# Delta-rule attention: the triangular inverse by 16-token substitution with a join on TensorE, both batches in step

## The chip, the cores and the metric

The program runs on one core of a Trainium2 chip. The metric is the device time of one execution in microseconds, measured over several runs; one further execution was profiled. A core has TensorE (PE in the rows, its weight loads PEld), VectorE (DVE), ScalarE (ACT), GpSimd (POOL) and SyncE (SP, which here only issues DMAs). Each engine executes its own instructions in program order and waits on semaphores for the others.

## The reference

Three stages follow each other. The change is in the first. For 2 batches, 8 heads, 768 tokens and 48 channels a state of 48x48 is updated token by token:

```
k_n = k / (norm(k) + 1e-06)
for t in range(768):
    y[t] = q[t] @ state
    state = state + beta[t] * outer(k_n[t], v[t] - k_n[t] @ state)
```

The second stage sends each token to one of 8 experts (the expert of the token before it is kept where a local gate says so) and applies a two-layer feed-forward network; the third is a gated feed-forward network with a convolution over 3 tokens.

## The kernel before, in words

**Blocks.** The 768 tokens are cut into 6 blocks of 128 (tb). Within a block the recurrence is solved at once: with the Gram matrix G of the keys, U = T (V - K S), where T is the inverse of a unit lower triangular matrix made of G and beta. Then the outputs are q S plus a masked Gram product M with U, and the state S gets K^T U. The 16 pairs of batch and head lie on the free axis; where a matrix product works on pairs, a batch b, a head pair i and a half e name one (hh = 8b + 4e + i).

**The inverse.** `solve` inverts the diagonal pieces of 32 tokens by substitution: the pieces are transposed so that 4 x 32 lanes each hold half of one head's row (lines 408 to 429), then 31 steps follow, each a multiply (line 435) and an add (line 437) on at most 136 elements a lane. Blocks 0, 2 and 4 run these steps on VectorE, blocks 1, 3 and 5 on GpSimd. The result is transposed back into Tn and Tt (lines 442 and 445). `merge1` and `merge2` (lines 462 and 475) join pairs of 32 into 64 on TensorE, 32 matmuls of 32x32 each; ScalarE takes the products out (lines 465 and 478).

**The recurrence in a block.** For each batch b: `s_ks` multiplies keys by the state (line 485), `s_r` forms V - K S for 64 tokens (line 504), `s_t` applies the 64x64 inverse (line 513, 8 matmuls on one quadrant of the array, ScalarE copies the result to U at line 515), `s_g` carries the first 64 tokens' U to the second half (line 521), and `s_r` and `s_t` follow for the second half. `s_qs` (line 492) and `s_m` (line 547) give the outputs, `s_s` (line 532) the new state, copied by ScalarE and VectorE (lines 537 and 539). `rows` (line 138) makes the gate's products of the finished block, `route1` to `route4` pick the expert, and an indirect DMA scatters the rows. Every fp32 matmul shows in the trace as two weight loads and two matmul records.

**Order.** The order of all pieces on all engines is written out by hand in the string ORDER: a letter is a piece, the digits its block, batch and half (J a Gram product, n a compaction of the diagonal pieces, A, B, C the start of a substitution, d one step, f its end, u and v the merges, K r t g q s the recurrence, m and x the output, a b e c the routing, w a warming matmul of 512 columns that keeps TensorE busy and gives no result). PSUM tiles of Gram products, merges, gate products and warming matmuls share a ring of 3 banks (tag gps). Loads of keys, queries and values are issued by SyncE ahead of the stage and once per block.

**After the stage** the second and third stages run as before; their first weights are loaded into buffers that the first stage leaves.

Of the kernel before, what the change touches and what calls it, by code (L numbers as in the profile page):

```python
# [9 lines left out]
I32 = mybir.dt.int32  # L10
# [22 lines left out]
THR = -1.5 * 2.0 ** -23  # L33

# [13 lines left out]
def hh_of(b, i, e):  # L48
    return 8 * b + 4 * e + i


class Router:
# [26 lines left out]
    def consts(self, ctx):  # L79
# [39 lines left out]
        self.xT, self.x = {}, {}  # L119
# [13 lines left out]
    def rows(self, tb, b, pg):  # L133

        nc = self.nc
        pt = pg.tile([128, 4, 2 * D + 9], F32, name="ptx", tag="gps")
        for i in range(4):
            nc.tensor.matmul(out=pt[:, i], lhsT=self.xT[b][:, i], rhs=self.wg[:, i], start=True, stop=True)
        if b == 0:
            self.lp = self.sb.tile([128, 2, 9], F32, name="lp", tag="lp", k=tb)  # L140
        nc.vector.tensor_reduce(out=self.lp[:, b], in_=pt[:, :, 2 * D:].rearrange("p i n -> p n i"), axis=AX.X, op=ALU.add)
        if b == 0:
            self.x[tb] = self.sb.tile([128, 2, XW], F32, name="x", tag="x", k=tb)
        x = self.x[tb][:, b, 0:DM]
        nc.scalar.copy(out=x.rearrange("p (i n) -> p i n", i=4), in_=pt[:, :, 0:2 * D])
        t0 = b * SEQ + tb * 128
        nc.sync.dma_start(out=self.xall[t0:t0 + 128, :], in_=x)

    def route1(self, tb, pg):
        nc, sb = self.nc, self.sb  # L150
        lp = self.lp
# [91 lines left out]
class Pieces:  # L243


    def __init__(self, gen):
        self.gen, self.left = gen, 31

    def setup(self):
        next(self.gen)  # L250

    def step(self):
        if self.left:
            next(self.gen)
            self.left -= 1

    def finish(self):
        while self.left:
            self.step()
        for _ in self.gen:  # L260
            pass


class Attention:
# [6 lines left out]
    def __init__(self, ctx, tc, kq, kn, vn, beta, wm):  # L271
# [16 lines left out]
        self.bt = con.tile([128, NTB, 32], F32, name="bt")  # L288
        self.mn = con.tile([128, NTB, 32], F32, name="mn")
        self.warm1 = con.tile([1, 1], F32, name="warm1")  # L290
        nc.vector.memset(self.warm1, 0.0)  # L291
        self.half = con.tile([128, 2], F32, name="half")
        self.ut = con.tile([128, 128], F32, name="ut")
        self.S = con.tile([128, 2, 4, 2, 64], F32, name="S")
        self.U2 = [[con.tile([128, 4, 2, 64], F32, name=f"U{b}{p}") for p in range(2)] for b in range(2)]
        self.sps = self.ps.tile([128, 2, 4, D], F32, name="sps")
        self.KQ, self.KN, self.VN, self.G, self.M, self.As, self.Tt, self.Tn = ({} for _ in range(8))
        self.W, self.Y, self.R, self.P = {}, {}, {}, {}

    def consts(self):  # L300
        nc = self.nc
        nc.scalar.activation(out=self.warm1, in_=self.warm1, func=AF.Sqrt)
        nc.gpsimd.memset(self.ut, 1.0)
        nc.gpsimd.affine_select(out=self.ut, in_=self.ut, compare_op=ALU.is_gt, fill=0.0, base=0,
                                pattern=[[1, 128]], channel_multiplier=-1)
        pi = self.con.tile([128, 1], I32, name="pi")
        nc.gpsimd.iota(pi, pattern=[[0, 1]], base=0, channel_multiplier=1)
        nc.vector.tensor_scalar(out=pi, in0=pi, scalar1=16, scalar2=None, op0=ALU.bitwise_and)
        nc.vector.tensor_scalar(out=self.half[:, 1:2], in0=pi, scalar1=-1.0 / 16, scalar2=None, op0=ALU.mult)
        nc.vector.tensor_scalar(out=self.half[:, 0:1], in0=self.half[:, 1:2], scalar1=-1.0, scalar2=-1.0, op0=ALU.mult, op1=ALU.add)  # L310
# [19 lines left out]
    def vhat(self, tb):  # L330
        m = self.mn[:, tb, 0:16].unsqueeze(2).to_broadcast([128, 16, D])
        self.nc.gpsimd.tensor_tensor(out=self.VN[tb], in0=self.VN[tb], in1=m, op=ALU.mult)

    def gram0(self, which, part):

        nc = self.nc
        dst = self.G if which == 0 else self.M
        if part == 0:
            p = self.gp if which == 0 else self.mp
            dst[0] = p.tile([128, 16, 128], F32, name="GM", tag="GM", k=0)  # L340
        if part % 2:
            return
        b = part // 2
# [17 lines left out]
    def gram(self, tb, part):

        nc = self.nc
        if part % 2:
            return
        if tb not in self.G:
            self.G[tb] = self.gp.tile([128, 16, 128], F32, name="GM", tag="GM", k=tb)
            self.M[tb] = self.mp.tile([128, 16, 128], F32, name="GM", tag="GM", k=tb)
        t = [self.pg.tile([128, 2, 2, 128], F32, name="gps", tag="gps") for _ in range(2)]
        b, i0 = part // 4, part % 4  # L370
# [4 lines left out]
        for e in range(2):  # L375
            h = slice(hh_of(b, i0, e), hh_of(b, i0, e) + 2)
# [10 lines left out]
    def compact(self, tb, q, eng):  # L387

        nc = self.nc
# [3 lines left out]
        o, i = self.As[tb][r], self.G[tb][r, :, 32 * q:32 * q + 32]  # L393
        if eng == "s":
            nc.scalar.copy(out=o, in_=i)
        else:
            {"v": nc.vector, "g": nc.gpsimd}[eng].tensor_copy(out=o, in_=i)

    def solve(self, tb):

        nc = self.nc
        up = self.up
        dve = tb % 2 == 0
        eng = nc.vector if dve else nc.gpsimd
        X = up.tile([128, 32, 16], F32, name="X", tag="X", k=tb)
        (nc.gpsimd if tb == 0 else eng).memset(X, 0.0)
        N = up.tile([128, 32, 32], F32, name="N", tag="N", k=tb)
        nc.vector.transpose(out=N.rearrange("p j (h u) -> p j h u", h=2),
                            in_=self.As.pop(tb).rearrange("p u j -> p j u").unsqueeze(2).to_broadcast([128, 32, 2, 16]))
        yield  # L410
        mu = up.tile([128, 32], F32, name="mu", tag="mu", k=tb)
        cu = up.tile([128, 32], F32, name="cu", tag="cu", k=tb)
        nu = up.tile([128, 32], F32, name="nu", tag="nu", k=tb)

        nc.scalar.activation(out=mu, in_=N.rearrange("p j i -> p (j i)")[:, ::33], func=AF.Sqrt)
        yield
        nc.vector.tensor_scalar(out=mu, in0=mu, scalar1=1e-6, scalar2=None, op0=ALU.add)
        nc.vector.reciprocal(out=nu, in_=mu)
        nc.vector.tensor_tensor(out=cu, in0=self.bt[:, tb], in1=nu, op=ALU.mult)
        nc.vector.scalar_tensor_tensor(out=cu, in0=cu, scalar=-1.0, in1=nu, op0=ALU.mult, op1=ALU.mult)  # L420
        for h in range(2):
            o = X.rearrange("p i l -> p (i l)")[:, 16 * h::33]
            if dve and tb > 0:
                nc.scalar.activation(out=o, in_=cu[:, h::2], func=AF.Copy, scale=self.half[:, h:h + 1])
            else:
                nc.gpsimd.tensor_scalar(out=o, in0=cu[:, h::2], scalar1=self.half[:, h:h + 1], scalar2=None, op0=ALU.mult)

        eng.tensor_tensor(out=N, in0=N, in1=cu.unsqueeze(2).to_broadcast([128, 32, 32]), op=ALU.mult)
        nc.vector.transpose(out=self.mn[:, tb], in_=mu)
        yield  # L430
        tm = up.tile([128, 136], F32, name="tm", tag="tm", k=tb)
        for j in range(31):
            n, m = 31 - j, j // 2 + 1
            t = tm[:, :n * m].rearrange("p (a b) -> p a b", b=m)
            eng.tensor_tensor(out=t, in0=N[:, j + 1:, j:j + 1].to_broadcast([128, n, m]),  # L435
                              in1=X[:, j:j + 1, :m].to_broadcast([128, n, m]), op=ALU.mult)
            eng.tensor_tensor(out=X[:, j + 1:, :m], in0=X[:, j + 1:, :m], in1=t, op=ALU.add)  # L437
            yield
# [702 lines left out]
```

## Time and profile before

| what | us |
|---|---|
| median of 3 runs | 504.63 (502.23 to 511.55) |
| the profiled execution's own time | 503.22 |
| its span, first to last instruction | 501.5 |
| PE busy | 455.2 (91%) |
| DVE busy | 362.8 (72%) |
| ACT busy | 240.4 (48%) |
| POOL busy | 175.4 (35%) |

Busy time is summed over the whole span, so it mixes stages; overlapping matmuls count once. PEclk is the clock that was granted to TensorE as a share of its full speed (1.00 is 2.4 GHz, 0.50 is 1.2 GHz).

### The profile page before, as it was taken

The numbers are of one execution on the slowest core, as the hardware profiler recorded it, in microseconds if no ns is written. First come the engines' busy times: TensorE is split into PE (matmuls) and PEld (weight loads), VectorE is DVE, ScalarE is ACT, GpSimd is POOL, SyncE is SP. The second block draws the span as 40 slices with busy tenths as digits, with TensorE's granted clock in tenths as the row PEclk, the third lists the DMA queues.
The fourth block names the chain that finished last, engine by engine and source line by source line (L and its number), as shares of the span: only waits on it lengthen the run. The fifth ranks groups of instructions, "written<-read, shape, count | busy, mean of one in ns | idle before, by whom it ended". The sixth has DMA issues, their size and how long they took to land. (4 is left out here: it accounts for less than half of the span.)

```text
span 501.5 us, 10035 instructions
## 1 busy us (share of the span) xinstructions
PE 455.2 (91%) x3980; PEld 403.4 (80%) x3982; DVE 362.8 (72%) x711; ACT 240.4 (48%) x435; POOL 175.4 (35%) x319
## 2 busy tenths in 40 slices
PE   7891998998997899988999999999999987999994
PEld 3551686976887698937999999999977987899993
DVE  3879669879669646464886799999812699965491
ACT  3772526347242314335656447546323764456541
POOL 5468828465548543230112202201210022222230
PEclk8787659679689958988999999999999999999998
DMA  9992020020220020169996788674008010002002
GB/s 278 367 371 84 3 61 5 18 80 2 64 67 33 35 95 33 66 225 347 293 316 228 258 314 290 223 256 158 33 31 283 2 33 31 1 0 95 1 1 101
DMA packets 44327, 64.97 MB, mean 130 GB/s; under 512 B 2480, under 2 KB 33456, under 8 KB 44272
## 3 DMA queue, kind: packets, MB, share of 16 engines
q1 hardware_dynamic: 42192, 58.38, 34.8%
q0 software_dynamic: 1792, 5.56, 2.9%
q8 instruction: 33, 0.54, 0.5%
q10 hardware_dynamic: 288, 0.31, 0.2%
q14 instruction: 22, 0.18, 0.1%
HBM read 48.38 MB, written 15.86 MB: 128 GB/s over the span
## 5 line engine op out<-in xcount | busy, mean ns | idle before, releaser
L750 POOL DMA_INDIRECT ys<-y,oi x16 | 25.8, 1615 | 126.5 <-ACT y L747 124.1
L666 DVE TENSOR_TENSOR wl<-raw,wh 128x1536 fp32r<-128x1536 f32 x32 | 56.1, 1754 | 5.2 <-ACT wh L665 5.1
L719 PE MATMUL ph<-xh,wh 128*128 128x256 f32 x192 | 55.1, 287 | 1.6 <-DVE hl L724 0.9
L719 PE MATMUL ph<-xl,wh 128*128 128x256 f32 x192 | 54.6, 285 | 0.3 <-DVE xl L689 0.3
L719 PE MATMUL ph<-xh,wl 128*128 128x256 f32 x192 | 54.6, 284 | 0.0
L928 POOL TENSOR_TENSOR ngl<-nc,ngh 128x768 fp32r<-128x768 f32 x13 | 25.6, 1968 | 82.5 <-ACT ngh L927 79.4
L940 PE MATMUL no<-wout,ngh 128*128 128x384 f32 x192 | 52.0, 343 | 0.0
L665 ACT CAST wh<-raw 128x1536 fp32r<-128x1536 f32 x32 | 47.2, 1475 | 4.9 <-DMA raw<-in_w_dram 4.9
L906 PE MATMUL npt<-nx,win 128*128 128x384 f32 (+1 forms) x243 | 44.2, 333 | 3.5 <-DVE nx L892 2.3
L906 PEld LDWEIGHTS npt<-nx,win 128*128 128x128 f32 x243 | 40.9, 188 | 4.5 <-DVE nx L892 2.7
L738 PE MATMUL py<-wh,hh 128*128 128x384 f32 x128 | 43.6, 341 | 0.0
L855 PE MATMUL warm<-wm 128*128 128x512 bf16 x121 | 40.4, 447 | 2.9 <-DVE warm L291 1.3
L738 PE MATMUL py<-wl,hh 128*128 128x384 f32 x128 | 43.0, 336 | 0.0
L738 PE MATMUL py<-wh,hl 128*128 128x384 f32 x128 | 43.0, 336 | 0.0
L437 POOL TENSOR_TENSOR X<-X,tm 128x126 f32<-128x126 f32 (+22 forms) x93 | 40.2, 432 | 7.3
L719 PEld LDWEIGHTS ph<-xh,wh 128*128 128x128 f32 x192 | 36.9, 192 | 2.4 <-DVE hl L724 1.3
L437 DVE TENSOR_TENSOR X<-X,tm 128x126 f32<-128x126 f32 (+22 forms) x93 | 36.1, 389 | 3.4
L435 POOL TENSOR_TENSOR tm<-N,X 128x126 f32<-128x126 f32 (+22 forms) x93 | 35.8, 385 | 6.2
L719 PEld LDWEIGHTS ph<-xh,wl 128*128 128x128 f32 x192 | 37.4, 195 | 0.0
L719 PEld LDWEIGHTS ph<-xl,wh 128*128 128x128 f32 x192 | 36.9, 192 | 0.5 <-DVE xl L689 0.5
L374 PE MATMUL gps<-kq 64*128 64x256 f32 x160 | 32.4, 471 | 4.7 <-ACT GM L359 3.2
L940 PEld LDWEIGHTS no<-wout,ngh 128*128 128x128 f32 x192 | 35.8, 193 | 0.1
(187 smaller groups left out, 1026.1 us busy)
## 6 DMA issues: line engine op xcount, KB each, us to landing
raw<-in_w_dram SPq DMA_DIRECT2D x32, 768.0 KB, 5.6
kq<-in_kq_dram SPq DMA_DIRECT2D x12, 512.0 KB, 6.5
xs<-S SPq DMA_DIRECT2D x1, 3144.0 KB, 14.6
xe<-xs SPq DMA_DIRECT2D x8, 393.0 KB, 6.9
raw<-in_win_dram SPq DMA_DIRECT2D x6, 512.0 KB, 7.4
raw<-in_wout_dram SPq DMA_DIRECT2D x8, 384.0 KB, 4.9
vn<-in_vn_dram SPq DMA_DIRECT2D x6, 384.0 KB, 3.3
kn<-in_kn_dram SPq DMA_DIRECT2D x6, 384.0 KB
```

The source lines that it names most:

```text
L374: nc.tensor.matmul(out=t[e][:, j], lhsT=kq[:, 0], rhs=kq, start=True, stop=True)
L435: eng.tensor_tensor(out=t, in0=N[:, j + 1:, j:j + 1].to_broadcast([128, n, m]), in1=X[:, j:j + 1, :m].to_broadcast([128, n, m]), op=ALU.mult)
L437: eng.tensor_tensor(out=X[:, j + 1:, :m], in0=X[:, j + 1:, :m], in1=t, op=ALU.add)
L665: nc.scalar.copy(out=h, in_=r)
L666: nc.vector.tensor_tensor(out=l, in0=r, in1=h.bitcast(F32), op=ALU.subtract)
L719: nc.tensor.matmul(out=p[:, j], lhsT=a[:, k, fs], rhs=c[:, k].rearrange("p c t -> p (c t)"), start=(n == 0), stop=(n == 8))
L738: nc.tensor.matmul(out=self.Y[c], lhsT=a[:, j, ts], rhs=w[:, f], start=(f2 == 0 and j == 0 and n == 0), stop=(f2 == 3 and j == 1 and n == 2))
L750: nc.gpsimd.indirect_dma_start(out=self.views[2 * e + c], out_offset=bass.IndirectOffsetOnAxis(ap=I[:, c:c + 1].bitcast(U32), axis=0), in_ ...
L855: nc.tensor.matmul(out=w, lhsT=wm[:, 0:128], rhs=wm, start=True, stop=True)
L906: nc.tensor.matmul(out=p, lhsT=a[:, k, fs], rhs=x[:, k, cs], start=(j == 0), stop=(j == 8))
L928: (nc.vector if (b, f) >= (1, 6) or (b, f) == (0, 0) else nc.gpsimd).tensor_tensor(out=gl, in0=c, in1=gh.bitcast(F32), op=ALU.subtract)
L940: nc.tensor.matmul(out=O[b, t], lhsT=a[:, ts], rhs=w[:, f], start=(f == 0 and j == 0), stop=(f == 7 and j == 2))
```

## The change

- Substitution runs on diagonal pieces of 16 tokens: 15 steps in place of 31, all on VectorE, at most 64 elements a lane for one block. Blocks are grouped as (0), (1, 2), (3, 4), (5); the two blocks of a group share their instructions. GpSimd runs no step.
- Two 16-token inverses are joined to 32 on TensorE: `join1` and `join2` are 64 matmuls each of one block, on the four diagonal 32x32 tiles of the array in turn, with one VectorE instruction between them. `merge1` and `merge2` follow as before.
- In keys, k and v of the second batch the two 64-token halves are swapped on the partitions. The first half of batch 0 lies on partitions 0 to 63, that of batch 1 on 64 to 127. `s_t` and `s_g` issue the matmuls of both batches alternately, `s_r` handles both batches in one instruction of 128 partitions, `s_ks` issues 8 matmuls with 64 weight columns in place of 4 with 128. ScalarE copies U of batch 0, VectorE of batch 1.
- G and M become one tile GM, taken out of PSUM by one copy in place of two; the ring holds 4 blocks in place of 5 and 4.
- ORDER is written anew: 60 warming pieces become 55, 15 of which stand at the end in both.

```diff
+GROUPS = [(0,), (1, 2), (3, 4), (5,)]
...
+def rows_of(g, b):
+    return slice(64, 128) if g ^ b else slice(0, 64)
...
-            nc.scalar.copy(out=self.G[tb][:, h], in_=t[e][:, :, 0])
-            nc.scalar.copy(out=self.M[tb][:, h], in_=t[e][:, :, 1])
+            nc.scalar.copy(out=self.GM[tb][:, h:h + 2], in_=t[e])
...
-        eng = nc.vector if dve else nc.gpsimd
...
-        for j in range(31):
-            n, m = 31 - j, j // 2 + 1
...
+    def step(self, gr, j):
+        nc = self.nc
+        g = len(GROUPS[gr])
+        N, X = self.N[gr], self.X[gr]
+        n, m = 15 - j, j + 1
...
+        nc.vector.tensor_tensor(out=t, in0=N[:, :, j + 1:, j:j + 1].to_broadcast([128, g, n, m]),
+                                in1=X[:, :, j:j + 1, :m].to_broadcast([128, g, n, m]), op=ALU.mult)
+        nc.vector.tensor_tensor(out=X[:, :, j + 1:, :m], in0=X[:, :, j + 1:, :m], in1=t, op=ALU.add)
+
+    def turn(self, tb):
...
+        nc.scalar.activation(out=F[:, 0], in_=X, func=AF.Copy, scale=self.h[:, 0:1])
+        nc.vector.tensor_scalar(out=F[:, 1], in0=X, scalar1=self.h[:, 1:2], scalar2=None, op0=ALU.mult)
...
+        nc.vector.transpose(out=Dn.rearrange("p s u l -> p l s u"), in_=F.rearrange("p s i l -> p l s i"))
+        nc.vector.transpose(out=Dt.rearrange("p u s i -> p i s u"), in_=F.rearrange("p s i l -> p i s l"))
...
+    def join1(self, tb):
...
+        for u in range(16):
+            for q in range(4):
+                r = slice(32 * q, 32 * q + 32)
+                nc.tensor.matmul(out=pp[r, u], lhsT=self.GM[tb][r, hh_u(q // 2, u), 0, r], rhs=Dn[r, 0, u], start=True, stop=True)
+        nc.vector.scalar_tensor_tensor(out=self.PI[:, :, 0:16], in0=pp, scalar=self.h[:, 2:3],
+                                       in1=self.eye[:, 0:16].unsqueeze(1).to_broadcast([128, 16, 16]), op0=ALU.mult, op1=ALU.add)
+
+    def join2(self, tb):
...
+                nc.tensor.matmul(out=po[r, u], lhsT=self.PI[r, u], rhs=Dt[r, u], start=True, stop=True)
+
...
+        nc.scalar.copy(out=Tt[:, :, 32:64], in_=po)
+        nc.scalar.activation(out=Tt[:, :, 0:32], in_=po, func=AF.Copy, scale=self.h[:, 3:4])
...
+        nc.vector.transpose(out=Tn, in_=Tt[:, :, 32:64])
...
+    def s_t(self, tb, g):
...
         for i in range(4):
             for e in range(2):
-                nc.tensor.matmul(out=self.W[b][r, i, e], lhsT=self.Tt[tb][r, hh_of(b, i, e)], rhs=self.R[b][r, i, e],
-                                 start=True, stop=True, skip_group_check=True)
-        nc.scalar.copy(out=self.U2[b][tb % 2][r, :, :, 0:D], in_=self.W[b][r])
...
+                for b in range(2):
+                    r = rows_of(g, b)
+                    nc.tensor.matmul(out=w[r, i, e], lhsT=self.Tt[tb][r, 8 * g + 4 * e + i], rhs=self.R[g][r, i, e],
+                                     start=True, stop=True, skip_group_check=True)
+        for b, copy in ((0, nc.scalar.copy), (1, nc.vector.tensor_copy)):
+            r = rows_of(g, b)
+            copy(out=self.U2[b][tb % 2][r, :, :, 0:D], in_=w[r])
```

VectorE, the end of block 0's substitution, before (tm and X the steps' tiles, Tn and Tt the inverse):

```order
L435 TENSOR_TENSOR tm<-N,X 128x30
L437 TENSOR_TENSOR X<-X,tm 128x2x15
L435 TENSOR_TENSOR tm<-N,X 128x16
L437 TENSOR_TENSOR X<-X,tm 128x16
L442 STREAM_TRANSPOSE Tn<-X 128x32x16
L445 STREAM_TRANSPOSE Tt<-Tn 128x16x32 x2
```

The same place now (F, Dn, Dt the turned 16-token inverses, pq the product of `join1`, PI the weights of `join2`, B and N_562 the start of the group of blocks 1 and 2):

```order
L452 TENSOR_TENSOR tm<-N_301,X_302 128x15
L454 TENSOR_TENSOR X_302<-X_302,tm 128x15
L463 TENSOR_SCALAR F<-X_302,halves 128x256
L466 STREAM_TRANSPOSE Dn<-F 128x16x32
L467 STREAM_TRANSPOSE Dt<-F 128x16x2x16
L479 SCALAR_TENSOR_TENSOR PI<-pq,halves,eye 128x16x16
L409 STREAM_TRANSPOSE B<-As 128x512
L413 SCALAR_TENSOR_TENSOR N_562<-B,halves,Bh 128x256
L495 STREAM_TRANSPOSE Tn<-Tt 128x512
```

The 31st step ended the substitution before and the 15th does now; behind it stand one scaling, two transposes, the product's scaling and, behind part of the next group's start, the transpose that `merge1` needs.

TensorE, from the first use of the state by block 1 to its first `s_t`, before (gps a Gram product, pps and pos the merges):

```order
L492 MATMUL y<-kq,S 128x128 x4
L485 MATMUL w<-S,kq 128x96 x4
L855 LDWEIGHTS wm
L855 MATMUL warm<-wm 128x512
L485 MATMUL w<-S,kq 128x96 x4
L462 MATMUL pps<-Tn,GM 32x32 x32
L374 MATMUL gps<-kq 128x256 x4
L475 MATMUL pos<-Tt,Pm 32x32 x32
L374 MATMUL gps<-kq 128x256 x4
L513 MATMUL w<-R_1036,Tt 64x48 x8
L513 MATMUL w<-R_1061,Tt 64x48 x8
```

The same place now (pq and poq the joins, of blocks 1 and 2 in turn):

```order
L529 MATMUL w<-S,kq 64x96 x8
L377 MATMUL gps<-kq 128x256 x4
L478 MATMUL pq<-Dn,GM 32x16 x64
L377 MATMUL gps<-kq 128x256 x4
L489 MATMUL poq<-Dt,PI 32x32 x64
L478 MATMUL pq<-Dn,GM 32x16 x64
L529 MATMUL w<-S,kq 64x96 x8
L505 MATMUL pps<-Tn,GM 32x32 x32
L489 MATMUL poq<-Dt,PI 32x32 x64
L152 MATMUL ptx<-wg,xT 128x105 x4
L516 MATMUL pos<-Tt,Pm 32x32 x32
L505 MATMUL pps<-Tn,GM 32x32 x32
```

The joins and first merges of two blocks stand together, and block 2's `merge1` too stands ahead of block 1's `s_t`.

TensorE, `s_g` of block 1, before:

```order
L521 MATMUL w<-U_127,GM 64x48 x8
L492 MATMUL y<-kq,S 128x128 x4
L521 MATMUL w<-U_125,GM 64x48 x8
L138 MATMUL ptx<-wg,xT 128x105 x8
L513 MATMUL w<-R_1036,Tt 64x48 x8
```

and now (the four rows of line 571 go on to 16, the two batches' tiles U in turn):

```order
L558 MATMUL w<-R_1071,Tt 64x48 x16
L537 MATMUL y<-kq,S 128x128 x4
L571 MATMUL w<-U_124,GM 64x48
L571 MATMUL w<-U_126,GM 64x48
L571 MATMUL w<-U_124,GM 64x48
L571 MATMUL w<-U_126,GM 64x48
```

Two runs of 8 matmuls, each on one quadrant of the array, have become one run of 16 that changes its quadrant with each matmul.

## Rows read from the trace of the kernel before

**Rows 1.** Busy time by stage: length, then PE, PEld, DVE, ACT, POOL; PEclk, DMA share, GB/s.
```profile
0.00:57.48 57.48, 40.42 (x313) 23.59 (x313) 44.20 (x105) 30.93 (x83) 37.66 (x95) 0.76 0.73 240
57.48:212.77 155.29, 144.15 (x1939) 125.11 (x1939) 110.29 (x285) 63.38 (x137) 81.80 (x177) 0.80 0.14 45
212.77:501.50 288.73, 270.63 (x1731) 254.68 (x1731) 208.28 (x321) 146.06 (x217) 55.97 (x48) 0.97 0.45 153
```

**Rows 2.** Timeline, PE and ACT, 39 to 58 us: start, length, instructions, wait before.
```profile
39.16 1.13 PE L374 MATMUL gps<-kq 64*128 64x256 f32 x6 [0.91 <-ACT GM L359]
49.70 1.91 PE L462 MATMUL pps<-Tn,GM 32*32 32x32 f32 x64 [9.42 <-DVE Tn L442]
...
51.65 1.19 ACT L465 ACTIVATE Pm<-pps 32x512 f32<-32x512 f32 x2 [10.55 <-PE pps L462]
...
55.11 1.70 PE L475 MATMUL pos<-Tt,Pm 32*32 32x32 f32 x64
```

**Rows 3.** Timeline of DVE, the substitution of block 0.
```profile
12.18 1.92 DVE L408 STREAM_TRANSPOSE N<-As 128x1024 f32<-128x1024 f32 x1
...
17.15 0.25 DVE L435 TENSOR_TENSOR tm<-N,X 128x31 f32<-128x31 f32 x1
...
22.75 0.26 DVE L435 TENSOR_TENSOR tm<-N,X 128x96 f32<-128x96 f32 x1
...
41.15 0.46 DVE L435 TENSOR_TENSOR tm<-N,X 128x96 f32<-128x96 f32 x1
...
48.47 1.09 DVE L442 STREAM_TRANSPOSE Tn<-X 128x512 f32<-128x512 f32 x1
```

**Rows 4.** Timeline of POOL, the first step of block 1's substitution.
```profile
32.04 0.25 POOL L435 TENSOR_TENSOR tm<-N,X 128x31 f32<-128x31 f32 x1
```

**Rows 5.** Groups of PE, 57.48 to 212.77 us: count, busy us, mean ns, idle before.
```profile
L513 PE MATMUL w<-R,Tt 64*64 64x48 f32 x384 | 32.4, 248 | 2.5 <-DVE R L504 1.3 <-ACT Tt L478 1.0
L521 PE MATMUL w<-U,GM 64*64 64x48 f32 x192 | 18.3, 263 | 1.5 <-ACT U L515 1.5
...
L374 PE MATMUL gps<-kq 64*128 64x256 f32 x64 | 10.5, 404 | 0.9 <-ACT GM L378 0.9
L855 PE MATMUL warm<-wm 128*128 128x512 bf16 x23 | 10.5, 475 | 0.0
L485 PE MATMUL w<-S,kq 128*128 128x96 f32 x80 | 10.3, 278 | 2.1 <-DVE S L539 2.1
L462 PE MATMUL pps<-Tn,GM 32*32 32x32 f32 x320 | 6.9, 201 | 2.2 <-DVE Tn L442 1.2 <-ACT GM L378 0.8
```

**Rows 6.** Timeline of PE, single pieces while the granted clock is 1.00.
```profile
147.16 2.05 PE L513 MATMUL w<-R,Tt 64*64 64x48 f32 x32 [0.31 <-DVE R L504]
...
159.23 0.92 PE L532 MATMUL sps<-U,kn 128*48 128x48 f32 x32
159.98 1.06 PE L547 MATMUL y<-GM,U 128*64 128x128 f32 x16
...
166.07 1.20 PE L462 MATMUL pps<-Tn,GM 32*32 32x32 f32 x64 [0.96 <-DVE Tn L442]
```

**Rows 7.** Timeline of PE where `s_g` meets `s_t` on another tile, clock 0.50.
```profile
180.72 1.62 PE L521 MATMUL w<-U,GM 64*64 64x48 f32 x13
182.05 0.34 PE L513 MATMUL w<-R,Tt 64*64 64x48 f32 x1
182.15 0.30 PE L521 MATMUL w<-U,GM 64*64 64x48 f32 x1
```

**Rows 8.** Busy time by stretch of half clock, columns as in rows 1.
```profile
59.80:73.40 13.60, 13.60 (x123) 10.96 (x123) 7.37 (x21) 3.85 (x8) 5.27 (x14) 0.50 0.10 30
...
90.50:107.60 17.10, 17.10 (x131) 15.48 (x131) 13.38 (x32) 5.13 (x12) 7.42 (x13) 0.50 0.15 47
...
128.00:141.70 13.70, 13.70 (x173) 12.39 (x173) 7.16 (x14) 4.33 (x8) 5.83 (x14) 0.50 0.15 45
...
175.80:192.90 17.10, 17.10 (x151) 15.66 (x151) 6.06 (x23) 3.44 (x8) 5.35 (x16) 0.50 0.21 70
```

More of the change, by code (lines that the diff above doesn't have):

```diff
@@ L240, in over @@
         return mi
[L243 to L261, printed above, removed]
 class Attention:
@@ L296, in __init__, with consts @@
         self.sps = self.ps.tile([128, 2, 4, D], F32, name="sps")
-        self.KQ, self.KN, self.VN, self.G, self.M, self.As, self.Tt, self.Tn = ({} for _ in range(8))
-        self.W, self.Y, self.R, self.P = {}, {}, {}, {}
-    def consts(self):
+        self.KQ, self.KN, self.VN, self.GM, self.As, self.Tt, self.Tn, self.N, self.X, self.D = ({} for _ in range(10))
+        self.W, self.Y, self.R, self.P, self.mu = {}, {}, {}, {}, {}
+    def consts(self, idn):
         nc = self.nc
         nc.scalar.activation(out=self.warm1, in_=self.warm1, func=AF.Sqrt)
[L303 to L310, printed above, removed]
@@ L336, in gram0 @@
         nc = self.nc
[L337 to L343, printed above, removed]
+        if 0 not in self.GM:
+            self.GM[0] = self.gp.tile([128, 16, 2, 128], F32, name="GM", tag="GM", k=0)
+        if which == 0 and part == 0:
+            self.As[0] = self.up.tile([128, 16, 32], F32, name="As", tag="As", k=0)
+        b = part
         ts = [self.pg.tile([128, 4, 128], F32, name="gps", tag="gps") for _ in range(2)]
@@ L392, in compact @@
         r = slice(32 * q, 32 * q + 32)
[L393 to L403, printed above, removed]
-        eng = nc.vector if dve else nc.gpsimd
[L405 to L416, printed above, removed]
+        for g in range(2):
+            b = g ^ (q // 2)
+            self.nc.scalar.copy(out=self.As[tb][r, 8 * g:8 * g + 8], in_=self.GM[tb][r, 8 * b:8 * b + 8, 0, 32 * q:32 * q + 32])
@@ L417, in solve @@
         nc.vector.tensor_scalar(out=mu, in0=mu, scalar1=1e-6, scalar2=None, op0=ALU.add)
         nc.vector.reciprocal(out=nu, in_=mu)
-        nc.vector.tensor_tensor(out=cu, in0=self.bt[:, tb], in1=nu, op=ALU.mult)
+        nc.vector.tensor_tensor(out=cu, in0=self.bt[:, t0:t0 + n], in1=nu, op=ALU.mult)
         nc.vector.scalar_tensor_tensor(out=cu, in0=cu, scalar=-1.0, in1=nu, op0=ALU.mult, op1=ALU.mult)
[L421 to L426, printed above, removed]
@@ L580, in attention @@
     A.warm(WARM0)
-    A.consts()
+    A.consts(R.idn)
     R.clear(A.S.rearrange("p b i e d -> p (b i e d)")[:, 0:XW], ys)
-    sol = [Pieces(A.solve(tb)) for tb in range(NTB)]
+    steps = [iter(range(15)) for _ in GROUPS]
     pieces = {
@@ L589, in attention @@
         "J": A.gram,
-        "k": lambda tb, p: A.mask(tb, p, MASK[p]),
-        "n": lambda tb, q: A.compact(tb, q, "s"),
-        "A": lambda tb: sol[tb].setup(),
-        "B": lambda tb: sol[tb].setup(),
-        "C": lambda tb: sol[tb].setup(),
-        "d": lambda tb: sol[tb].step(),
-        "f": lambda tb: sol[tb].finish(),
+        "k": A.mask,
+        "n": A.compact,
+        "A": A.diag,
+        "B": A.norms,
+        "C": A.scale,
+        "E": A.means,
+        "d": lambda gr: A.step(gr, next(steps[gr])),
+        "f": A.turn,
+        "o": A.join1,
+        "p": A.join2,
         "u": A.merge1,
         "v": A.merge2,
-        "z": A.zero,
         "l": A.load_n,
```

221 lines of the change are left out of this document (139 added, 82 removed), and 26 rows, old and new, of the table ORDER.

## The prediction

> **What bounds the kernel now.** I read the busy times by stage first. The change is in the first stage, so the third line of [rows 1] (288.7 us, PE 270.6) is taken as it is: all that comes after the last gate product at 212.77 us starts from it and moves with it. The first stage has two parts. In the first 57.48 us PE is busy for 40.4 us; from there to 212.77 us, the part in which the recurrence runs, PE is busy for 144.2 of 155.3 us, DVE for 110.3, ACT for 63.4 [rows 1]. So the second part is bound by PE, with 11.1 us of waits in it, and a shorter DVE chain there earns nothing by itself.
>
> The timeline shows why the first part is long. PE has finished the Gram products that it may make and waits 9.42 us for Tn, the end of block 0's substitution, before the first merge at 49.70 [rows 2]. That substitution runs on DVE from 17.15 to 48.47 us, 31 steps of two instructions, and it slows on the way: the same 128x96 multiply takes 0.26 us at 22.75 and 0.46 at 41.15 [rows 3], after POOL has begun its own substitution at 32.04 [rows 4]. The first `s_t` stands at 57.48, the border in [rows 1].
>
> Third, how PE spends its time. The costliest group is `s_t`, 32.4 us, then `s_g`, 18.3 [rows 5]. Both issue all their matmuls to one quadrant. At full clock 32 records of `s_t` take 2.05 us, 64 ns each, while 32 records of `s_s`, which change the column half with every matmul, take 0.92, 29 ns each; 16 records of `s_m` with 64 weight columns and 128 moving ones, also alternating, take 1.06, and 64 records of `merge1` on two tiles take 1.20, 19 ns each [rows 6]. So the pace follows the wider of weights and moving operand, and matmuls on disjoint tiles share it. A border of two pieces says the same: a record of the following `s_t` starts at 182.05, 0.10 us ahead of a record of `s_g` that stands before it in the program [rows 7].
>
> Last, the clock: 0.80 on the mean in the second part [rows 1], since four stretches of 13.6, 17.1, 13.7 and 17.1 us run at 0.50 [rows 8]. That is 61.5 of 155.3 us, a share of 0.40. During the first of them PE did short matmuls on quarters of the array; the idle 9.42 us too lie in a stage with a clock of 0.76.
>
> **Part one: the start of the recurrence.** Before, the substitution's transpose stood at 12.18, the steps began at 17.15, Tn's transpose at 48.47, the first `s_t` at 57.48. Now:
> - Three more warming matmuls and one more Gram piece stand ahead of the second half of block 0's Gram product: six records of such a piece took 1.13 us [rows 2], and its copies hold the ring. Estimate: the transpose starts at 15.8, 3.6 later (0 to 5).
> - From there to the first step 5.0 us, as before (12.18 to 17.15); the transposed data are half as much, but two instructions are added.
> - 15 steps are 30 instructions at 0.25 to 0.26 us [rows 3], with pauses some 7.6 us; one copy, one small transpose and two masks between them some 1.9. The slow rows are not used, for POOL runs no steps now. Steps end at 30.3 instead of 48.5.
> - One scaling 0.4, Dn's transpose 1.1 (as Tn's in [rows 3]), `join1` 1.6, its scaling 0.6, `join2` 1.6, ACT's copy 0.6 (half of 1.19 in [rows 2]), Tn's transpose 1.1, and 0.2 for each of three changes of engine: 37.9.
> - `merge1` 1.2 [rows 6], ACT 1.19, `merge2` 1.1, ACT again 1.2, changes of engine 0.8, pieces between 0.9: the first `s_t` at 44.5.
> That is 13 us earlier. Bounds: 39 and 50, so 18 to 7 us.
>
> **Part two: PE's work from the first `s_t` to the last gate product,** against the rows of the mixed clock [rows 5]:
> - `s_t` and `s_g` alternate between disjoint quadrants: by `s_s` against `s_t` they halve, 32.4 + 18.3 = 50.7, so 25.4 less. Bounds: 0 (no sharing) and 27.
> - `s_ks` has twice the matmuls with half the weight columns, alternating. Its 96 moving columns stand between `s_s` (48 columns, 29 ns) and `s_m` (128, 66 ns): some 49 ns by 16 records against 129 by 8, so 10.3 us fall by 2.4 (0 to 4).
> - 8 warming matmuls of 23 are left there: 10.5 x 15 / 23 = 6.8 less. They cost what PE, the bound, would otherwise do; where PE would wait anyway they were free, so the bound is 2.
> - One more Gram piece falls into this part (9 for 8): 10.5 / 8 = 1.3 more.
> - `join1` and `join2` of five blocks are 640 matmuls of 32 columns. `merge1` took 6.9 us for 160 (320 records), 43 ns each, on two tiles in turn: 27.6 if no more than two share, 13.8 if all four do. The overtaking in [rows 7] speaks for four, a fixed cost for each record against it; I take 18.
> - Waits: before, 11.1 us. Chains in a block are as long as before and have fewer pieces to fill them. In the second order place, `merge1` of block 1 needs Tn, and DVE does one scaling, two transposes, an R and a mask of the next block ahead of it; that is some 4 us against some 4 us of PE work. I take 5 more (4 less to 14 more).
> - POOL's substitution (all of which lay beside PE's work), half of the Gram copies' overhead and the zeroing on ACT go: nothing on the path. DVE falls from 110 to some 102 us of a shorter stage: the steps lose some 18, copies of U add 6.6.
> Sum: -25.4 - 2.4 - 6.8 + 1.3 + 18 + 5 = -10.3, so 155.3 becomes 145.0 at the same share of half clock. At full clock that is 145.0 x 0.80 = 116.
>
> **The clock.** The paired quadrants do more in a time, the joins on 32x32 tiles and the loss of warming matmuls do less. I take a share of 0.44 at half clock in place of 0.40: 116 / 0.78 = 148.7. Bounds: 0.25 gives 133, 0.55 gives 160.
>
> The last gate product then ends at 44.5 + 148.7 = 193.2 instead of 212.8, 19.6 earlier; the profiled execution's 503.2 us becomes 483.6. It lies 1.4 below the median of the runs, so the forecast for the median is 485.
>
> **A rule against the change.** 64 records of `merge1` in 1.20 us are one in 19 ns [rows 6]. The Trainium skill, "TensorE: Matmul & The Clock Gate", section "Wait — 56ns, not 53.3ns?", has it that matmul starts never follow each other by less than about 25 ns however small they are. The trace goes under that with two tiles in turn. By that rule four tiles would earn nothing and the joins would cost 640 x 2 x 25 ns = 32 us at full clock in place of 18. The same skill, "TensorEngine Tiling (Array Packing)", section "Key Properties", says that different tiles load and multiply in parallel; by that the joins cost the lower 13.8.
>
> **The rivals.**
> 1. Starts of records have a floor, so that matmuls of 32 columns gain nothing from four tiles. At the pace of `s_s`, 29 ns [rows 6], 1280 records take 37 us in place of 18, and the two joins of block 0 in the start 4 more: 508. Against: `merge1` itself runs at 19 ns. Chance 0.05. The first rule above is of this kind.
> 2. Waits take PE's place. Both batches in step leave nothing of the other batch to do while U or R is copied, and the copies of U, R and S stand on DVE behind transposes of 1.1 us. Five blocks with 3 us each more: 500. For it: DVE is busy for 71% in [rows 1]. Against: of the 11.1 us of waits only few were for R and U [rows 5]. Chance 0.16.
> 3. The quadrants do not share (the change does not do what it says): the 25.4 us stay, 510. [Rows 6, 7] speak against it. Chance 0.05.
> 4. PE falls to half clock for most of the part: 116 us of work on small tiles with no warming matmuls between. At a share of 0.70 the part takes 116 / 0.65 = 178 and ends at 223, so 515; it becomes slower than before from a share of 0.62 (116 / 0.69 = 168.3, 44.5 + 168.3 = 212.8). For it: [rows 8] begin behind short matmuls. Against: half of the part would have to be worse than any long piece of before. Chance 0.06.
> 5. All four tiles share and the clock holds (share 0.30): (145.0 - 4.2) x 0.80 / 0.85 = 132.5, end at 177, 469. Chance 0.12.
>
> **How the numbers follow.** The forecast, 474 to 496, has 0.56. The range 470 to 501 leaves out most of rivals 3 and 4 and a part of 5, some 0.17 in all. Faster by over 2% (below 494.5, about what a measurement of this kernel tells from no change): nearly all of the forecast, rival 5 and a third of rival 2, 0.71. Slower by over 2% is most of rival 4: 0.06. The rest, 0.23, lies within 2%.
>
> **What would show it.** First `s_t` between 40 and 49 us, with 30 step instructions at about 0.25 us. 32 records of `s_t` in about 1.1 us at full clock; if 2.0, rival 3. A join in 1.1 to 1.7 us at full clock; if 3 to 4, rival 1. Waits of PE between first `s_t` and last gate product under 20 us; if 30, rival 2. A mean clock there between 0.73 and 0.85; under 0.69, rival 4. Stages two and three unchanged within 3 us; if not, the step that was wrong is the one that takes them as they are.

## The result and the profile after

The changed kernel takes 487.56 us in the median of 4 runs (483.66 to 496.76), the kernel before 505.43 (502.23 to 511.55): the ratio is 0.9641, 95% interval 0.9538 to 0.9744. The ratio leaves out executions that show a lower clock and take over 1.5% longer than the fastest of their kernel (here 496.76). The forecast was 485. The profiled execution, the fastest of the four, took 483.66 us, its span 482.0.

Busy time by stage after the change, columns as in [rows 1]; the borders are again the first `s_t` and, to 0.2 us, the end of the last gate product:

```profile
0.00:53.10 53.10, 39.68 (x564) 25.30 (x564) 26.60 (x80) 28.95 (x64) 14.48 (x52) 0.84 0.88 260
53.10:192.50 139.40, 121.42 (x3295) 106.83 (x3294) 89.25 (x259) 61.48 (x128) 26.39 (x41) 0.85 0.16 51
192.50:482.00 289.50, 269.42 (x1738) 253.32 (x1736) 208.72 (x321) 146.79 (x217) 56.83 (x49) 0.98 0.45 152
```

Against [rows 1] the first part lost 4.4 us (13 were forecast), the second 15.9 (6.6 were forecast), the third grew by 0.8. So the end of the last gate product, 192.5, is the 193.2 of the forecast, out of two parts that are both wrong. The records of PE in the second part went from 1939 to 3295, and its mean clock from 0.80 to 0.85.

PE's groups in the second part, columns as in [rows 5], busy us and mean ns, then the idle time before them:

```profile
L558 PE MATMUL w<-R,Tt 64*64 64x48 f32 x384 | 16.0, 241 | 0.4 <-DVE R L547 0.4
...
L529 PE MATMUL w<-S,kq 128*64 128x96 f32 x160 | 10.8, 288 | 2.8 <-DVE S L589 1.9 <-issue 0.8
L489 PE MATMUL poq<-Dt,PI 32*32 32x32 f32 x640 | 9.9, 215 | 5.2 <-issue 5.1
...
L478 PE MATMUL pq<-Dn,GM 32*32 32x16 f32 x640 | 7.9, 188 | 6.0 <-issue 4.9 <-ACT GM L380 0.7 <-DVE Dn L466 0.4
L516 PE MATMUL pos<-Tt,Pm 32*32 32x32 f32 x320 | 7.5, 206 | 0.5 <-issue 0.5
L571 PE MATMUL w<-U,GM 64*64 64x48 f32 x192 | 7.0, 220 | 0.0
```

`s_t` and `s_g` (L558, L571) fell from 50.7 to 23.0 us. The joins (L478, L489) cost 17.8. New is an idle time that the rows put down to "issue": 11.8 us in which PE waits for no semaphore that the profile shows, 10.0 of them before or inside joins. Single pieces at full clock, to be read against [rows 6], a `s_g`, a `s_t` and a `join1`:

```profile
114.45 1.15 PE L571 MATMUL w<-U,GM 64*64 64x48 f32 x32
...
117.69 1.13 PE L558 MATMUL w<-R,Tt 64*64 64x48 f32 x32
...
120.27 1.25 PE L478 MATMUL pq<-Dn,GM 32*32 32x16 f32 x128 [0.38 <-DVE Dn L466]
```

A `s_t` takes 1.13 us where it took 2.05, and 128 records of a join take 1.25, one in 9.8 ns. Now a place where joins are cut in two, blocks 1 and 2 on PE's timeline (start, length, last column the wait before):

```profile
74.91 0.70 PE L489 MATMUL poq<-Dt,PI 32*32 32x32 f32 x58
76.45 0.79 PE L489 MATMUL poq<-Dt,PI 32*32 32x32 f32 x70 [0.83 <-issue]
77.09 0.67 PE L478 MATMUL pq<-Dn,GM 32*32 32x16 f32 x58
80.30 1.08 PE L478 MATMUL pq<-Dn,GM 32*32 32x16 f32 x70 [2.54 <-issue]
```

Between the two waits PE ran 70 + 58 = 128 records of matmuls, with their weight loads 256 instructions. The page's list of DMA queues has the other half of it:

```profile
q8 instruction: 46, 0.75, 0.7%
```

46 packets of 16 KB, for 5593 matmuls and as many weight loads: one packet for some 243 of them (33 packets before the change). All nine waits over 0.7 us without a semaphore come at the same count of PE instructions modulo 256 (193 or 194, its semaphore instructions counted), and end 1.3 to 1.5 us after the end of a packet of this queue; the packet of the wait at 80.30 ran from 77.84 to 78.89.

The stretches of half clock, which answer to [rows 8]:

```profile
43.10:56.60 13.50, 13.38 (x201) 10.34 (x199) 6.59 (x17) 7.63 (x15) 1.60 (x4) 0.50 0.05 17
80.50:97.50 17.00, 15.43 (x453) 14.35 (x441) 7.22 (x18) 6.93 (x14) 0.00 (x0) 0.50 0.20 62
124.80:138.50 13.70, 11.01 (x344) 9.89 (x339) 5.03 (x12) 4.38 (x9) 2.48 (x5) 0.50 0.11 38
165.80:172.60 6.80, 6.69 (x203) 6.36 (x202) 4.76 (x14) 2.15 (x4) 1.64 (x2) 0.50 0.03 8
```

From the first `s_t` on they are 3.5 + 17.0 + 13.7 + 6.8 = 41.0 of 139.4 us, a share of 0.29, where 0.44 was forecast. Each begins behind joins with a wait in them.

The start, PE, then DVE:

```profile
9.64 1.23 PE L377 MATMUL gps<-kq 64*128 64x256 f32 x8 [2.31 <-DMA kq<-in_kq_dram]
...
15.06 1.61 PE L355 MATMUL gps<-kq 64*128 64x128 f32 x15 [2.49 <-DMA kq<-in_kq_dram]
...
33.86 1.13 PE L377 MATMUL gps<-kq 64*128 64x256 f32 x6 [2.52 <-ACT GM L380]
34.91 1.36 PE L478 MATMUL pq<-Dn,GM 32*32 32x16 f32 x128
36.21 2.08 PE L377 MATMUL gps<-kq 64*128 64x256 f32 x8
38.22 1.18 PE L489 MATMUL poq<-Dt,PI 32*32 32x32 f32 x71
42.14 0.69 PE L489 MATMUL poq<-Dt,PI 32*32 32x32 f32 x57 [2.75 <-issue]
...
45.40 1.92 PE L505 MATMUL pps<-Tn,GM 32*32 32x32 f32 x64
```
```profile
14.44 1.03 DVE L409 STREAM_TRANSPOSE B<-As 128x512 f32<-128x512 f32 x1
...
18.16 0.49 DVE L413 SCALAR_TENSOR_TENSOR N<-B,halves,Bh 128x256 f32<-128x256 f32 x1 [2.69 <-ACT Bh L412]
20.03 0.18 DVE L427 TENSOR_SCALAR mu<-mu 128x16 f32<-128x16 f32 x1 [1.38 <-ACT mu L419]
...
21.52 0.18 DVE L452 TENSOR_TENSOR tm<-N,X 128x15 f32<-128x15 f32 x1
...
22.87 1.53 DVE L452 TENSOR_TENSOR tm<-N,X 128x48 f32<-128x48 f32 x1
24.44 0.21 DVE L454 TENSOR_TENSOR X<-X,tm 128x48 f32<-128x48 f32 x1
...
31.68 0.17 DVE L454 TENSOR_TENSOR X<-X,tm 128x15 f32<-128x15 f32 x1
...
32.50 1.08 DVE L466 STREAM_TRANSPOSE Dn<-F 128x512 f32<-128x512 f32 x1 [0.25 <-ACT F L462]
```

PE stands behind the loads of `J10` and `i1` in its own queue (`J` is a Gram product of a later block, `j` and `i` block 0's, of keys with keys and of keys with queries); one instruction of the substitution takes 1.53 us instead of 0.2; each join stands behind a Gram piece; the second join waits 2.75 us for instructions, and `merge1` runs at half clock.

### The profile page after: what moved, and what is told of

It is laid out like the page before. It is cut to its first block, busy times and chain, and to the rows that moved or that the text cites. A ratio compares the mean times of both kernels' runs of the same rounds, so it can differ in the third digit from the quotient of the medians.

```text
span 482.0 us, 12973 instructions
## 1 busy us (share of the span) xinstructions
PE 430.5 (89%) x5593; PEld 385.4 (80%) x5593; DVE 324.6 (67%) x659; ACT 237.2 (49%) x409; POOL 97.7 (20%) x142
## 3 DMA queue, kind: packets, MB, share of 16 engines
q1 hardware_dynamic: 42192, 58.38, 37.1%
## 5 line engine op out<-in xcount | busy, mean ns | idle before, releaser
L900 PE MATMUL warm<-wm 128*128 128x512 bf16 x118 | 31.9, 402 | 3.8 <-DVE warm L286 1.2
L377 PE MATMUL gps<-kq 64*128 64x256 f32 x160 | 29.1, 464 | 5.8 <-ACT GM L380 2.8
L985 PE MATMUL no<-wout,ngl 128*128 128x384 f32 x96 | 32.9, 343 | 0.6 <-POOLq L1138 0.6
L768 ACT ACTIVATE hh<-ph 128x512 fp32r<-128x512 f32 x32 | 19.2, 599 | 22.8 <-PE ph L764 22.4
L959 DVE SCALAR_TENSOR_TENSOR nc<-nh,convw,nc 128x768 f32<-128x768 f32 x16 | 17.1, 1067 | 18.9 <-ACT nc L958 18.9
```

Of the source, the lines that this page charges most:

```text
L377: nc.tensor.matmul(out=t[e][:, j], lhsT=kq[:, 0], rhs=kq, start=True, stop=True)
L768: nc.scalar.activation(out=h, in_=p, func=AF.Relu)
L900: nc.tensor.matmul(out=w, lhsT=wm[:, 0:128], rhs=wm, start=True, stop=True)
L959: nc.vector.scalar_tensor_tensor(out=c, in0=h[:, 1:S + 1], scalar=cw[:, f, 1:2], in1=c, op0=ALU.mult, op1=ALU.add)
L985: nc.tensor.matmul(out=O[b, t], lhsT=a[:, ts], rhs=w[:, f], start=(f == 0 and j == 0), stop=(f == 7 and j == 2))
```

## The experiments

Every kernel is the changed one with one edit. "Part two" is the stretch from the first `s_t` to the end of the last gate product, 139.4 us in the changed kernel.

**Unpaired quadrants.** In `s_t` and `s_g`:

```
-        for i in range(4):
-            for e in range(2):
-                for b in range(2):
+        for b in range(2):
+            for i in range(4):
+                for e in range(2):
```

> Both s_t and s_g issue the 16 matmuls of one batch and then those of the other, so that neighbours use the same quadrant; the arithmetic is the same. Theory (disjoint quadrants share the array): 32 records of s_t go from 1.13 to about 2.0 us at full clock, as in the kernel before; 18 such pieces x 0.9 = 16 us more at full clock, and the stretch from the first s_t to the last gate product goes from 139.4 to 150-160 us (a part of it is taken back, because slower pieces leave fewer waits inside the joins). Rival (the gain came from the clock or from the new order): 32 records stay at 1.13 us and the stretch stays within 3 us of 139.4.

Part two took 157.4 us, 18.0 more, at a clock of 0.78. The one execution took 508.6 us, the whole gain gone; but 6.8 us of that lie in the third part, which the edit does not touch (296.3 us for 289.5).

```profile
L558 PE MATMUL w<-R,Tt 64*64 64x48 f32 x384 | 29.1, 254 | 0.0
...
L571 PE MATMUL w<-U,GM 64*64 64x48 f32 x192 | 14.0, 249 | 0.0
```
```profile
123.56 1.87 PE L558 MATMUL w<-R,Tt 64*64 64x48 f32 x32
```

32 records take 1.87 us at full clock for 1.13, as the theory has it. The quadrants do share the array: 43.1 us against 23.0. By the full-clock pieces 13.3 of these 20.1 us are the sharing (18 pieces); the rest goes with the lower clock.

**Joins on two tiles in turn.** In both joins:

```
-        for u in range(16):
-            for q in range(4):
+        for u2 in range(32):
+            for q in (2 * (u2 // 16), 2 * (u2 // 16) + 1):
+                u = u2 % 16
```

> The joins issue their matmuls so that only two of the four 32x32 tiles alternate. If four tiles share the array, a join without a wait in it goes from 1.25 to about 1.9-2.4 us at full clock (two tiles: 19 ns a record, or less sharing). Theory A (PE waits in the joins for its instructions: the waits without a semaphore end 1.3-1.5 us after a packet of the instruction queue, and all stand at the same count of PE instructions modulo 256): the waits shrink by about what the joins grow, so the stretch from the first s_t to the last gate product stays within 3 us of 139.4. Theory B (the waits are something that four tiles in turn cause): the waits vanish, and they do not come back at the same counts.

```profile
125.44 2.11 PE L479 MATMUL pq<-Dn,GM 32*32 32x16 f32 x128 [0.39 <-DVE Dn L466]
```

A join without a wait takes 2.11 us at full clock, so four tiles share. In part two the joins grew from 17.8 to 27.0 us, the waits for instructions shrank from 11.8 to 5.4 and came at the same counts. But part two took 150.3 us, 10.9 more and not within 3: its clock was 0.79, and `s_t` with `s_g` took 26.7 for 23.0. Theory A is right that the waits shrink and keep their counts, though by 6.4 us where the joins grew by 9.2; neither theory had the clock in it.

**No joins.** One matmul stands for each join's 64:

```
-        for u in range(16):
-            for q in range(4):
...
+        nc.tensor.matmul(out=pp, lhsT=self.GM[tb][:, 0, 0], rhs=Dn[:, 0], start=True, stop=True)
```

> Each join's 64 matmuls are replaced by one matmul of 128 columns on the whole array, so the product that joins the two halves of 32 tokens is left out; all copies, transposes and waits for semaphores stay. Theory A: the ten joins after the first s_t cost 17.8 us of PE and 11.8 of waits without a semaphore, so the stretch from the first s_t to the last gate product goes from 139.4 to about 108-116 us, no wait without a semaphore over 0.5 us is left there, and the half-clock stretches that begin right behind such a wait go too. Theory B (the waits only fill time in which PE would have waited for DVE and ACT anyway): the stretch falls by 10 us or less and the waits turn up as waits for Tn, R or U.

Only part two can be read, for with other values the later stages do other work. It took 116.4 us, just over theory A's range, with no wait for instructions, and its clock is the surprise:

```profile
50.23:166.60 116.37, 103.84 (x2035) 86.15 (x2034) 88.67 (x259) 60.92 (x128) 25.77 (x41) 0.98 0.18 59
```

0.98 for 0.85. The matmuls that stand in for the joins take 8.9 us, so the joins with all that follows from them cost 139.4 - 116.4 + 8.9 = 32 us, of which 17.8 are their own busy time and 11.8 their waits. The rest is a balance: at the higher clock PE's other work took 8.9 us less, and waits for DVE and ACT rose from 6.0 to 12.2 us, which is what theory B has in a smaller size.

**Blocks of 256 instructions in a row,** behind the last piece of the order:

```
+    for m in (0, 12):
+        for _ in range(12):
+            pp = A.pg.tile([128, 512], F32, name="pz", tag="gps")
+            for u in range(16):
+                for q in range(4):
+                    r = slice(32 * q, 32 * q + 32)
+                    nc.tensor.matmul(out=pp[r, 16 * u:16 * u + 16], lhsT=A.ut[r, r], rhs=A.ut[r, 16 * (u % 8):16 * (u % 8) + 16], start=True, stop=True)
+            if m:
+                A.warm(m)
```

> Behind the attention part 24 blocks of 64 matmuls of 32x32 tiles by 16 columns (256 PE instructions each, weights loads counted) are added: 12 without anything between, then 12 with 12 matmuls of 512 bf16 columns behind each. Nothing reads them. Theory A (instructions come in blocks of 256, and no block can be done sooner than about 3.85 us after the one before was entered): the first 12 take 12 x 3.6 to 4.0 = 43-48 us, with one wait of 2.3 to 2.7 us in each and packets of the instruction queue 3.6-4.0 us apart; the second 12 have no such wait over 0.3 us. Theory B (the waits belong to what the joins read or write): the first 12 take 12 x 1.25 = 15 us at full clock, up to 30 at half clock, without waits.

This execution ran at half clock nearly throughout (mean 0.55), so a block's matmuls take 1.9 us where a join took 1.25, and the waits, 1.2 to 2.1 us, are shorter than the 2.3 to 2.7 expected. The period is about the same at full clock: the waits at 76.45 and 80.30 in the changed kernel end 3.85 us apart. Three blocks of the first kind and two of the second:

```profile
250.78 1.90 PE L673 MATMUL pz<-ut 32*32 32x16 f32 x128 [1.55 <-issue]
254.23 1.90 PE L673 MATMUL pz<-ut 32*32 32x16 f32 x128 [1.55 <-issue]
257.69 1.90 PE L673 MATMUL pz<-ut 32*32 32x16 f32 x128 [1.55 <-issue]
...
297.45 1.63 PE L673 MATMUL pz<-ut 32*32 32x16 f32 x128
299.02 4.71 PE L909 MATMUL warm<-wm 128*128 128x512 bf16 x12
303.66 1.70 PE L673 MATMUL pz<-ut 32*32 32x16 f32 x128
```

The first 12 last from 240.5 to 286.2 us, one every 3.45 to 4.0 us with a wait in each; they read one constant tile, and nobody reads what they write. With 4.7 us of other work behind each block there is no wait. Theory A holds.

**POOL beside the steps.** In `step`:

```
+        if gr == 0:
+            s = self.U2[1][1][:, 0:2]
+            for _ in range(2):
+                nc.gpsimd.tensor_tensor(out=s, in0=s, in1=s, op=ALU.mult)
```

> Beside each step of block 0's substitution on DVE, POOL gets two multiplies of 128x256 elements on a tile that holds zeros. Theory (the steps of the kernel before slowed from 0.26 to 0.46 us because POOL ran its own substitution beside them): the 128x96 multiply and those near it take 0.35 to 0.5 us instead of 0.26 (0.20 for the block's 16x16 tiles), and the 30 instructions some 3 us more in all. Rival (POOL does not matter): 30 instructions with the same durations as in the kernel after the change, 0.17 to 0.23 us, but for single ones.

```profile
32.39 0.66 DVE L452 TENSOR_TENSOR tm<-N,X 128x64 f32<-128x64 f32 x1
33.08 0.66 DVE L454 TENSOR_TENSOR X<-X,tm 128x64 f32<-128x64 f32 x1
```

Beside 0.71 us a multiply on POOL (20 in 14.21 us), nearly every step instruction of DVE takes 0.66 instead of 0.22, more than the 0.35 to 0.5 expected, and the steps end at 43.65 us instead of 31.85 (2.8 us of it a wait for POOL's `vn`). So DVE does not slow by a fixed factor: its instruction takes about as long as the POOL instruction beside it. The same can be read in the two other kernels on POOL's timeline, beside the 0.46 us step of [rows 3] at 41.15 and, after the change, beside the 1.53 us step at 22.87:

```profile
41.06 0.43 POOL L435 TENSOR_TENSOR tm<-N,X 128x126 f32<-128x126 f32 x1
```
```profile
22.86 1.48 POOL L341 TENSOR_TENSOR vn<-vn,mn 128x768 f32<-128x768 f32 x1
```

**The start, twice.** First, `j1` and the diagonal blocks before `J10`, and `i1` behind `J23`:

```
-w*3 j0 J10 j1 i1 A0 J11
+w*3 j0 j1 A0 J10 J11
...
-n11 q00 k010 d0
+n11 q00 d0
...
-J22 J23 n20 o0
+J22 J23 i1 n20 o0
...
-J33 k011 B1
+J33 k011 k010 B1
```

> Only the order of the start differs: j1 and the diagonal blocks of block 0 come before J10, i1 and its mask move behind J23, into the time in which PE waits for Dn. Theory (the head's 8.6 us over the forecast come in part from PE standing behind the loads of J10 and i1 in its own queue, 2.3 and 2.5 us): block 0's transpose starts at about 12 instead of 14.4 us, the first s_t 2 to 4 us earlier than 53.1, and the end the same 2 to 4 us earlier, 480 to 482 us in the profiled run. Rival (the head is set by something that is not moved: the load of the keys, the joins' instructions, the half clock from 43 us): the first s_t moves by less than 1 us.

The transpose of block 0 moved from 14.44 to 11.94 us and Dn from 32.50 to 29.19, but the first `s_t` only from 53.10 to 52.26: `join1`, free to start at 30.3, started at 33.48, behind `J23` and `i1`, which waited for ACT's copies. That is the rival's under 1 us, though the theory's loads did hold the transpose back. 485.45 us (478.52 to 486.09), ratio 0.9564 (0.9429 to 0.9699): not told from the changed kernel. Then with `i1` and its masks (`k`) behind the first `s_t`, in place of five of eight warming matmuls:

```
-t00 d1 J31 d1*2 g0 r01 k211 w d1 q01 d1*2 k000 w k300 w n30 w t01 w*2 k111 k001 d1 n31 w*2 d1*4 m00
+t00 d1 J31 d1*2 g0 r01 k211 i1 d1 q01 d1*2 k000 k300 w n30 t01 w k011 k111 k001 k010 d1 n31 w d1*4 m00
```

> The start as in e5_head (j1 and the diagonal blocks before J10), but i1 and its two masks stand behind the first s_t, where eight warming matmuls were (two of them are left). In e5_head the transpose of block 0 came 2.5 us earlier and Dn 3.3 us, and i1, put right before join1, took that back. Theory: join1 of block 0 starts at 30 to 31.5 us instead of 34.9, the first s_t at 48 to 50.5 instead of 53.1, the last gate product 2 to 4 us earlier than 192.5, the kernel 482 to 486 us. Rival: the first s_t comes earlier, but the part behind it gets longer by as much (masks and i1 in it, or a lower clock), and the end stays at 192.

`join1` started at 31.59 and the first `s_t` at 47.87, 5.2 us earlier, the last gate product ended at 188.1, 4.4 earlier. 480.47 us (478.46 to 483.81), ratio to the kernel before 0.9577 (0.9474 to 0.968). The theory holds and its rival does not, though all four numbers lie a little outside the theory's ranges; by the ratios alone this kernel is not told from the changed one.

**Another order, three times.** Joins and merges spread between pieces of few, long matmuls. Blocks 1 and 2 in the last of the three:

```
-J41 K10 J42 h1 o1 n33 f2 r10 J43 n40 k410 k400 p1 n41 o2 n42 K11 n43 A3 u1 A4 p2 x01 B2 C2 v1 l2 u2 t10
+J40 q10 K10 d1 l2 f1 J41 k111 o1 J42 A3 J43 k211 k310 p1 n40 x00 x01 r10 f2 h2 u1 a0 k400 n41 n42 n43 v1 o2 A4 t10
```

> Another order of the pieces from the first s_t on, the same pieces otherwise: joins and merges, which have many short instructions, are put between Gram pieces, gate products and s_qs, which have few and long ones, so that 256 PE instructions seldom take under 3.85 us of work. Theory A (the waits in the joins are for instructions, and the half-clock stretches begin behind them): the waits without a semaphore fall from 11.8 to under 4 us, half clock behind the first s_t falls from 41 us to under 20, the stretch to the last gate product from 139.4 to 115-125 us, and the kernel takes 463 to 473 us. Theory B (the new order makes chains wait instead, or the clock falls for other reasons): stretch 135-145 us, no faster than the kernel after the change.

492.26 us (486.24 to 496.35): no gain, as theory B has it. Waits for instructions in part two fell to 2.8 us, but part two took 139.7, with 38.9 us at half clock. Its order also had 21 warming matmuls in that part for 9, 7.7 us for 2.5, and PE waited 3.2 us before them for a PSUM buffer.

> Both orders, the start of the one and the rest of the other. If the two gains lie in stretches that follow each other, they add: 2 to 4 us below the run with the spread order alone, 460 to 470 us. If the spread order only moves waits, it is as fast as the better of the two.

490.94 us (488.81 to 491.71): the starts did not add, for the first `s_t` stood at 52.7 again, part two took 138.9, and the 21 warming matmuls were still there. What both runs lost on the changed kernel lies for the most part behind part two: their third parts took 298.0 and 298.3 us for 289.5. Behind the last piece these orders leave 2 warming matmuls of 19; in the first 22.5 us of the third part PE was busy for 12.4 and 12.3 us for 19.4, at a clock of 0.84 and 0.85 for 1.00. That the missing warming matmuls did this was not shown by a run of its own.

> The start of e9_head2 and a spread order of the pieces from the first s_t on, this time with none of the warming matmuls behind s0 (e7_both had 21 of them in that part, 13 more than the kernel after the change, at 0.38 us and up, and three waits of theirs). Theory A: waits without a semaphore inside joins under 6 us, half clock behind the first s_t 20 to 30 us, stretch from first s_t to last gate product 125 to 133 us, kernel 470 to 478 us. Theory B (joins on small tiles lower the clock with or without waits in them, and what the waits lose the clock takes): half clock 40 us or more, stretch 136 to 142 us, kernel 480 to 488 us.

471.31 us (469.90 to 474.22), ratio 0.9377 (0.9306 to 0.9448): faster than both kernels. Against the kernel with the second start alone, which begins the same way, part two went from 140.2 to 131.6 us:

```profile
48.33:179.90 131.57, 121.08 (x3306) 106.16 (x3305) 89.74 (x265) 63.37 (x132) 26.45 (x42) 0.87 0.16 55
```
```profile
PE pps L505 <- issue: 0.9, 2, 0.5
PE pq L478 <- issue: 0.7, 2, 0.5
PE poq L489 <- issue: 0.4, 1, 0.4
PE w L571 <- issue: 0.4, 1, 0.4
```

The waits for instructions are 2.4 us where they were 11.8 with the same start: 9.4 us of waits for 8.6 of time. PE's busy time stayed (121.1 us for 121.4) and its other waits rose by 1.2, so the waits cost about their own length, as far as a run can show it that moves all other pieces too. Most of the half clock stayed: 6.8 + 13.7 + 13.7 = 34.2 us, over the 20 to 30 of theory A, where it was 41.0 with the same start. The third part took 292.4 us; this order has 22 warming matmuls behind its last piece.

## Why the prediction was right, and where it was wrong

The total was right by luck: two steps failed by nearly the same amount in opposite directions, 8.6 us late and 9.3 us short.

- **The start failed:** first `s_t` at 53.1, forecast 44.5 (its terms add up to 44.3), bounds 39 to 50. The steps ended 1.5 us late (31.85 for 30.3). The transpose stood 1.4 us earlier than forecast, but the way to the first step took 7.1 us for 5.0, with 4.1 us of waits for ACT in it, and the steps 10.3 for 9.5. The one that stood beside POOL's multiply cost 1.3 of that: "POOL runs no steps now" was not the same as POOL doing nothing there. From the steps to the end of `join2` it took 11.0 us, by the forecast's terms 5.7. Of the 5.3 more, 2.75 are the wait for instructions, a cost that no term had, and 2.5 are Gram pieces that stand ahead of the joins in PE's queue: `join1` could have started at 33.6 and did at 34.91, `join2` at 37.1 and did at 38.22. The rest of the way took 10.3 us at half clock for 8.5; the run with the second start took 7.55 for the same pieces at mostly full clock, so the half clock is the whole of that miss.
- **Sharing was right:** 27.7 us less for 25.4, a little over the bound of 27. The unpaired run puts 20.1 of it on the pairing, its clock included; the 7.6 us between that run and the kernel before were not taken apart. Rival 3 is out.
- **The joins' own time was right:** 17.8 us for 18, 1.25 us each for "1.1 to 1.7". With their waits and what they do to the clock they cost 32. The Trainium skill, "TensorE: Matmul & The Clock Gate", section "Wait — 56ns, not 53.3ns?", sets starts no closer than about 25 ns; the trace has 9.8 ns with four tiles in turn, so rule and rival 1 do not hold here.
- **The waits had the right size and the wrong cause:** 139.4 - 121.4 = 18.0 us, forecast 16.1. Named were Tn and DVE; 11.8 of them are instructions, and of the chain's only S (1.9) and U (1.4) stand out. By the forecast's own sign, under 20 us, rival 2 did not come.
- **The clock failed in sign:** a share at half clock of 0.29 for 0.44. At 0.29 the forecast's 116 us would have made 135.7 instead of 148.7, so this step alone took off 13.0 us, and the other terms together were 3.7 too low. Both halves of the reason are borne out by single runs: with paired quadrants the clock is higher (0.85, unpaired 0.78), with joins it is lower (0.85, without them 0.98). The runs with the two starts and with POOL beside the steps, whose part two is nearly the same, have 0.84, 0.85 and 0.88, so both differences are larger than what one execution differs from another here. But 0.07 up and 0.13 down do not give a rise from 0.80 to 0.85: something else in the change raised the clock too, if such effects add, and no run takes it apart. Why the chip grants what it grants was not settled.
- **Two terms too low:** `s_ks` took 10.8 us where the forecast makes 7.9 of it. At full clock 16 of its records take 0.88 us, 55 ns each for the 49 forecast; the rest is that three of its pieces now lie in stretches of half clock. The merges, which had no term, went from 13.2 to 16.0. In the run without joins, at a clock of 0.98, `s_ks` took 8.5 and the merges 12.0.
- **DVE and the rest:** 89.25 us of DVE for 102, off the path as told. The third part took 289.5 for 288.7, within the 3.

## What to carry to other kernels

When a change splits matmuls into many small ones, count PE's instructions, weight loads too, as well as its busy time: one join's 256 passed in 1.25 us, but when such bursts followed each other, a block of 256 took 3.45 to 4.0 us. Put such bursts next to pieces of few, long matmuls, and look in the timeline for waits without a semaphore in the middle of a piece. A total that comes out right shows little until each of its stretches has been compared.

## What was not expected of the hardware

**Instructions have a rate.** One packet of 16 KB comes for some 243 PE instructions, and the waits repeat every 256; in a row a block every 3.45 to 4.0 us is the most that PE got, 27 to 31 ns for a matmul with its load, while the array did a join's at 9.8. The Trainium skill, "Runtime: NRT & Kernel Launch", section "Instruction fetch mechanics", tells of the blocks of 256 and has the cost of their borders as mostly hidden. The trace agrees on the blocks, not on the cost: 11.8 us of 139.4.

**A DVE instruction can take as long as the POOL instruction beside it.** 0.66 us instead of 0.22 beside POOL multiplies of 0.71, and 1.53 beside one of 1.48. The Trainium skill, "SBUF — State Buffer", section "Who interferes with whom", has it that a DVE instruction with two SBUF inputs and a POOL instruction that reads SBUF lock each other out; the run agrees.
